# Emitting an attention-and-MoE kernel's own plan under the framework's manual schedule

## The chip, the core and the metric

One core of one Trainium2 chip. The time is device microseconds of one execution of the program, from its first to its last instruction with what the launch adds around them; the median of several executions counts. The engines are named as in the profile: PE (matmuls; PEld is its weight loads), DVE (vector), ACT (scalar), POOL and SP, of which SP issues nearly all input transfers and POOL some.

## The reference

Two stages, all in float32. First an attention over 32 memory slots, for 8 batches of 8 heads with 576 tokens of 64 elements:

```python
a = softmax(phi, over tokens)                    # phi: 8 x 8 x 576 x 32
k_m, v_m = a^T k, a^T v                          # 32 x 64 for each head
attn = softmax(q k_m^T / 8, over the 32 slots)
x = attn v_m                                     # to 4608 x 512
```

Then a feed-forward layer on the 4608 rows: `h = x @ w_in` (512 to 2048), `g = relu(h)**2`, and `out = g @ w_out` (2048 to 512).

## The kernel before

**The work.** The kernel never forms x. For each batch and each slice of 256 columns of w_in it multiplies v_m into w_in once (the tile `vw`; L679 for batches 0 and 1, L698 for the others), so that `h = attn @ vw`. A number that must be exact to float32 is kept as a high and a low part, each in the reduced-width float32 type of the matmuls, and each product is three matmuls: high by high, high by low, low by high. So each `h` tile is evacuated by several steps: relu into `r` (L811 on ACT or L812 on DVE), the high part `gh` of its square (L813, ACT), the square itself in `r` (L815 ACT or L816 DVE), and the low part `glo` (L817, DVE). The last 64 of the 576 tokens go the same way through the small tiles `gl` (L814 on ACT, L818 on DVE). The second product adds `gh` and `glo` times w_out into four PSUM banks `acc` (L842, L843 with `gh`; L845 with `glo`), and the 64 tokens left over of two batches into `accl` (L868).

**A step** is one batch and one block of 128 of the 2048 hidden columns: 12 matmuls of `h` (tile `h{step}_1` has 320 tokens, `h{step}_0` has 256) and 12 of `acc`. There are 8 x 16 steps. For batches 2 to 7, two batches form a pair n = 1, 2, 3. In the first batch of a pair every second step also makes a slice s = 0 to 7 of `vw` for both batches: two groups of six matmuls, `pvw{n}_{s}_0` and `pvw{n}_{s}_1` (`vw_step`, L689). Both groups write the same single PSUM bank (tag `pv`), so the second must wait until the first has been read out of it. The reading out is four copies on ACT (L328, called with `src`) and four subtractions on DVE (L707), each on 64 of the 128 partitions:

```python
pw = pt("pv", f"pvw{n}_{s}_{hh}")
...
op({"PE": 720}, mm, [t, vh, vl], [pw], lead=True)
for hf in (0, 1):
    pr = slice(64 * hf, 64 * hf + 64)
    for x in (0, 1):
        ...
        op({"ACT": act(SL)}, ..., [pw], [(V, (hh, 0, hf))], lead=True)
        vec({"DVE": tt(SL)}, ..., [pw, (V, (hh, 0, hf))], [(V, (hh, 1, hf))], ...)
```

**The start** is different. The weights come as 8-byte numbers, and 32 pieces of 512 KB (`raw`, L402) are decoded into high and low parts by a chain that goes back and forth between DVE (L404, L406, L407, L409, L418) and ACT (L405, L408, L328). A raw buffer is loaded again when its L409 has run. The decoding runs beside the steps of batches 0 and 1, up to about 200 us.

**What sets the order.** The kernel doesn't emit its instructions as it builds them. Each is an `Op` of a `Plan` (class at L58) with a cost on each engine that could take it and with the ops on which it depends. `plan.order()` schedules all ops on a model of five engines and a DMA wire, forward and backward in turns, and gives a list sorted by planned start (`o.start`). The costs are formulas such as `tt(n) = 68 + 1.04 n` ns for a DVE operation on n columns and `act(n) = 35 + 0.96 n` on ACT; a reader of a tile depends on its writer, but two readers of one tile don't depend on each other. The ops are then emitted in that list's order (L977). Under the framework's ordinary mode, this order is only the priority with which the framework's scheduler lists each engine's instructions, by a model of its own; it may put an instruction behind later ones. The framework sets all semaphores. It also lets no two engines use one PSUM bank at the same time, in the order in which the accesses were emitted.

**Fillers.** Where the plan sees PE idle before an op, `fill` (L350) emits matmuls on a tile of zeros, one for each 360 ns of the planned gap. They write the bank `idle` (L354) or, when `acc` is in use, add zero to a live bank (L356). There are 54 of them, nearly all before the first step.

Of the kernel before, what the change touches and what calls it, by code (L numbers as in the profile page):

```python
# [33 lines left out]
FILL = 360.0  # L34
# [240 lines left out]
def tile_attention_moe(  # L275
# [41 lines left out]
    plan = Plan()  # L317
# [32 lines left out]
    def fill(n):  # L350

        for _ in range(n):
            if idle is not None and not live:
                nc.tensor.matmul(idle, zero.broadcast_to([P, P]), zero.broadcast_to([P, 512]), start=True, stop=True)  # L354
            elif live:
                nc.tensor.matmul(live[min(live)](), zero.broadcast_to([P, P]), zero.broadcast_to([P, 512]), start=False, stop=False)  # L356
# [3 lines left out]
                            fill=0.0, base=0, channel_multiplier=1)  # L360
    nc.gpsimd.affine_select(out=bd, in_=bd, pattern=[[32, 4]], compare_op=ALU.is_ge,
                            fill=0.0, base=31, channel_multiplier=-1)
# [611 lines left out]
        for ff in range(NFF):  # L974
            step(pos[b1, ff])

    for o in plan.order():  # L977
        if o.left == "PE":
            fill(int(o.gap / FILL))
        o.fn(o.left)  # L980


# [28 lines left out]
```

## Time and profile before

| | us |
|---|---|
| median of 3 runs (all) | 807.02 (806.92, 807.02, 810.13) |
| the profiled execution | 805.84 |
| its span, first to last instruction | 804.0 |
| PE busy | 769.0 (96%) |
| DVE busy | 570.4 (71%) |
| ACT busy | 376.8 (47%) |
| mean granted PE clock | 0.983 |

The profiled execution is 1.84 us longer than its span, and 1.18 us shorter than the median of the runs. PE's busy time is a union of overlapping matmuls, so small stalls between two matmuls do not show in it; they show in the distance between two starts, or in the chain that ended last, where a piece reaches from one end to the next. In timeline rows the columns are start, duration, engine, line, operation and tiles, with the count, and in square brackets the engine's idle time before it and what ended that. Tile names in the profile have no numbers.

### The profile page before, as it was taken

To read this page: it belongs to the slowest core of one execution; us is meant where nothing else is said; L and a number is where in the kernel's file an instruction comes from. 1 tells how busy PE (TensorE), PEld (TensorE's weight loads), DVE (VectorE), ACT (ScalarE), POOL (GpSimd) and SP (SyncE) were. 2 spreads that over 40 slices of the span, in tenths; PEclk is the share of its full clock that TensorE was granted. 3 is DMA by queue.
4 is the path that set the end of the run, shared out by engine and by line. 5 is a ranking of instruction groups with operands and counts; after the bars stand their busy time and mean duration, and the time that the engine had idled before them with its cause. 6 is when DMAs were issued, how large, how long until landed. Compare 5 with 4: busy or idle time off the path is not lost.

```text
span 804.0 us, 13239 instructions
## 1 busy us (share of the span) xinstructions
PE 769.0 (96%) x4944; PEld 652.0 (81%) x4944; DVE 570.4 (71%) x1262; ACT 376.8 (47%) x857; POOL 54.1 (7%) x95
## 2 busy tenths in 40 slices
PE   9678899999999999999999999999999999999994
PEld 5467788888788888888888888888888888888883
DVE  3897988895659667966669667967759667974541
ACT  1566676675454444532443444533444444542220
POOL 4111102120100100010000100010000100000000
PEclk9789999999999999999999999999999999999998
DMA  6976754566554333421454523421424523110001
GB/s 194 291 243 227 247 185 156 206 217 185 164 142 134 119 99 97 126 50 52 125 152 123 132 88 98 136 52 38 120 82 112 139 82 104 31 34 20 1 8 58
DMA packets 91779, 97.89 MB, mean 122 GB/s; under 512 B 23812, under 2 KB 79108, under 8 KB 91716
## 3 DMA queue, kind: packets, MB, share of 16 engines
q1 hardware_dynamic: 82980, 81.55, 34.3%
q0 software_dynamic: 8736, 15.50, 6.6%
q8 instruction: 39, 0.64, 0.3%
q14 instruction: 24, 0.20, 0.1%
HBM read 79.17 MB, written 17.83 MB: 121 GB/s over the span
## 4 chain that ended last, share of the span: by engine, by line
PE 81%; DMA 7%; DVE 5%; ACT 4%; issue 1%; SPq 0%; ACTq 0%; DVEq 0%
PE h L807 22%; PE acc L842 13%; PE acc L845 13%; PE acc L843 13%; PE accl L868 5%; PE pvw L698 5%; DMA raw<-in_moe_w_out_dram 3%; PE psc L736 3%; PE pkv L484 3%; DMA raw<-in_moe_w_in_dram 2%; PE idle L354 1%; PE pvw L679 1%; DMA phi<-in_phi_dram 1%; ACT vw L328 1%; DVE vw L707 1%
## 5 line engine op out<-in xcount | busy, mean ns | idle before, releaser
L807 PE MATMUL h<-ath,vw 128*128 128x256 f32 (+1 forms) x1024 | 212.1, 302 | 2.9 <-ACT r L811 1.7
L842 PE MATMUL acc<-wo,gh 128*128 128x512 f32 x512 | 207.3, 406 | 2.1 <-ACT wo L328 1.0
L843 PE MATMUL acc<-wo,gh 128*128 128x512 f32 x512 | 201.7, 395 | 0.0
L807 PEld LDWEIGHTS h<-ath,vw 128*128 128x128 f32 x1024 | 171.4, 191 | 17.7 <-ACT r L811 2.2
L845 PE MATMUL acc<-wo,glo 128*128 128x512 f32 x512 | 155.3, 397 | 1.6 <-DVE glo L817 1.6
L842 PEld LDWEIGHTS acc<-wo,gh 128*128 128x128 f32 x512 | 96.7, 189 | 22.4 <-ACT gh L813 1.5
L328 ACT CAST vw<-pvw 64x256 fp32r<-64x256 f32 (+1 forms) x202 | 73.4, 378 | 85.2 <-PE pvw L698 55.9
L807 PE MATMUL h<-atl,vw 128*128 128x320 f32 (+1 forms) x512 | 111.2, 297 | 0.0
L813 ACT ACTIVATE gh<-r 128x512 fp32r<-128x512 f32 x128 | 80.8, 631 | 64.9 <-DVE r L812 53.2
L843 PEld LDWEIGHTS acc<-wo,gh 128*128 128x128 f32 x512 | 96.8, 189 | 16.3
L845 PEld LDWEIGHTS acc<-wo,glo 128*128 128x128 f32 x512 | 91.0, 189 | 17.2 <-DVE glo L817 2.6
L812 DVE TENSOR_SCALAR r<-h 128x256 f32<-128x256 f32 (+1 forms) x125 | 56.0, 448 | 60.4 <-PE h L807 59.5
L707 DVE TENSOR_TENSOR vw<-pvw,vw 64x256 fp32r<-64x256 f32 x192 | 78.5, 419 | 26.6 <-ACT vw L328 23.5
L817 DVE TENSOR_TENSOR glo<-r,gh 128x512 fp32r<-128x512 f32 x128 | 87.4, 683 | 6.4 <-ACT r L815 3.7
L811 ACT ACTIVATE r<-h 128x320 f32<-128x320 f32 (+1 forms) x131 | 53.7, 413 | 66.4 <-PE h L807 65.0
L807 PEld LDWEIGHTS h<-atl,vw 128*128 128x128 f32 x512 | 83.3, 191 | 0.4
L814 ACT ACTIVATE gl<-r 128x64 fp32r<-128x64 f32 x128 | 32.5, 254 | 78.6 <-DVE r L812 76.9
L816 DVE TENSOR_TENSOR r<-r 128x576 f32<-128x576 f32 x53 | 40.1, 757 | 26.7 <-ACT gh L813 24.3
L868 PE MATMUL accl<-wo,gl 128*128 128x512 f32 x192 | 53.0, 393 | 0.0
L815 ACT ACTIVATE r<-r 128x576 f32<-128x576 f32 x75 | 51.3, 684 | 1.8
L868 PEld LDWEIGHTS accl<-wo,gl 128*128 128x128 f32 x192 | 35.0, 188 | 7.2 <-ACT o L328 0.5
L698 PE MATMUL pvw<-wi,VTh 128*128 128x256 f32 x192 | 38.8, 292 | 1.5 <-issue 0.8
(142 smaller groups left out, 839.4 us busy)
## 6 DMA issues: line engine op xcount, KB each, us to landing
wi<-w_in_hi SPq DMA_DIRECT2D x56, 256.0 KB
wi<-w_in_lo SPq DMA_DIRECT2D x56, 256.0 KB
KV<-in_k_dram SPq DMA_DIRECT2D x32, 256.0 KB
KV<-in_v_dram SPq DMA_DIRECT2D x32, 256.0 KB
raw<-in_moe_w_in_dram SPq DMA_DIRECT2D x16, 512.0 KB
raw<-in_moe_w_out_dram SPq DMA_DIRECT2D x16, 512.0 KB
q<-in_q_dram SPq DMA_DIRECT2D x24, 288.0 KB
out_dram<-o POOLq DMA_DIRECT2D x20, 256.0 KB, 7.9
```

The source lines that it names most:

```text
L328: nc.scalar.copy(o, i) if e == "ACT" else ENG[e].tensor_copy(o, i)
L698: nc.tensor.matmul(pw()[:, x * SL:(x + 1) * SL], l()[:, 2 * hh + x, :], w(r, x), start=(i == 0), stop=(i == 2))
L707: vec({"DVE": tt(SL)}, lambda e, V=V, pr=pr, src=src: nc.vector.tensor_sub(V()[pr, 1, hh, :], src(), V()[pr, 0, hh, :].bitcast(F32)), [pw, ...
L807: nc.tensor.matmul(p()[:, 0:n], V()[:, l, hh, c0:c0 + P], x()[:, hh, cs], start=(i == 0), stop=(i == 5))
L811: op({"ACT": act(n), **({} if b < 2 else {"DVE": tt(n)})}, lambda e, cs=cs, n=n, p=p: nc.scalar.activation(r()[:, cs], p()[:, 0:n], AF.Rel ...
L812: else nc.vector.tensor_scalar(r()[:, cs], p()[:, 0:n], 0.0, None, ALU.max), [p], [(r, h)])
L813: op({"ACT": act(SM)}, lambda e: nc.scalar.activation(gh(), r()[:, 0:SM], AF.Square), [r], [gh])
L817: vec({"DVE": tt(SM)}, lambda e: nc.vector.tensor_sub(glo(), r()[:, 0:SM], gh().bitcast(F32)), [r, gh], [glo])
L842: nc.tensor.matmul(a(), gh()[:, c], t()[:, 0], start=f0, stop=False)
L843: nc.tensor.matmul(a(), gh()[:, c], t()[:, 1], start=False, stop=False)
L845: nc.tensor.matmul(a(), glo()[:, c], t()[:, 0], start=False, stop=f1)
L868: nc.tensor.matmul(a(), G()[:, l, :], t()[:, w], start=(ff == 0 and n == 0), stop=(ff == NFF - 1 and n == 2))
```

## The change

One `with` is put around the emission. The instructions, their engines, their tiles and their data dependences are the same; what changes is who orders them. Each engine now gets its instructions in the order in which they are emitted, which is the plan's.

```diff
-    for o in plan.order():
-        if o.left == "PE":
-            fill(int(o.gap / FILL))
-        o.fn(o.left)
+    with tc.manual_schedule():
+        for o in plan.order():
+            if o.left == "PE":
+                fill(int(o.gap / FILL))
+            o.fn(o.left)
```

Three places show what moves. **PE between the two `pvw` groups** of slice 4 in pair 1 (steps 38 and 39; `vw`, `ath` and `atl` are the operands of `h`). Before, from the last two `acc` matmuls that follow `pvw1_4_0` to the first row of `pvw1_4_1`:

```order
L845 MATMUL acc2_0_0_3118<-wo21_1098,glo37_3399 128x512
L845 MATMUL acc2_0_1_3128<-wo21_1098,glo37_3399 128x512
L807 MATMUL h38_1_3433<-ath2_2933,vw1_0_3_3305 128x320 x2
L807 MATMUL h38_1_3433<-atl2_2978,vw1_0_3_3305 128x320 x2
L807 MATMUL h38_1_3433<-ath2_2933,vw1_0_3_3305 128x320 x2
L807 MATMUL h38_0_3450<-ath2_2933,vw1_0_3_3305 128x256 x2
L807 MATMUL h38_0_3450<-atl2_2978,vw1_0_3_3305 128x256 x2
L807 MATMUL h38_0_3450<-ath2_2933,vw1_0_3_3305 128x256 x2
L845 MATMUL acc2_0_2_3135<-wo21_1098,glo37_3399 128x512
L845 MATMUL acc2_0_3_3156<-wo21_1098,glo37_3399 128x512
L807 MATMUL h39_1_3468<-ath2_2933,vw1_0_3_3305 128x320 x2
L698 MATMUL pvw1_4_1_3441<-wi1_4_1_3307,VTh10_2336 128x256 x2
```

The same place on PE under the plan's order:

```order
L845 MATMUL acc2_0_0_3120<-wo21_1100,glo37_3401 128x512
L845 MATMUL acc2_0_1_3130<-wo21_1100,glo37_3401 128x512
L807 MATMUL h38_1_3435<-ath2_2935,vw1_0_3_3307 128x320 x2
L807 MATMUL h38_1_3435<-atl2_2980,vw1_0_3_3307 128x320 x2
L807 MATMUL h38_1_3435<-ath2_2935,vw1_0_3_3307 128x320 x2
L698 MATMUL pvw1_4_1_3443<-wi1_4_1_3309,VTh10_2338 128x256 x2
L698 MATMUL pvw1_4_1_3443<-wi1_4_1_3309,VTl10_2344 128x256
```

The second group now stands ten matmuls earlier: the six of `h38_0`, two of L845 and the first two of `h39_1` are behind it instead of ahead. Ahead of these rows stand four matmuls of L842 and L843 right behind `pvw1_4_0`, in both orders. The same move stands at slices 3, 4, 5 and 6 of all three pairs, twelve times.

**DVE at the same place**, from the first subtraction that reads `pvw1_4_0`. Before:

```order
L707 TENSOR_TENSOR vw1_0_4_3417<-pvw1_4_0_3408,vw1_0_4_3417 64x256
L707 TENSOR_TENSOR vw1_1_4_3423<-pvw1_4_0_3408,vw1_1_4_3423 64x256
L812 TENSOR_SCALAR r38_3448<-h38_1_3433 128x320
L707 TENSOR_TENSOR vw1_1_4_3423<-pvw1_4_0_3408,vw1_1_4_3423 64x256
L707 TENSOR_TENSOR vw1_0_4_3417<-pvw1_4_0_3408,vw1_0_4_3417 64x256
L812 TENSOR_SCALAR r38_3448<-h38_0_3450 128x256
L812 TENSOR_SCALAR r39_3490<-h39_1_3468 128x320
```

And under the plan's order:

```order
L707 TENSOR_TENSOR vw1_0_4_3419<-pvw1_4_0_3410,vw1_0_4_3419 64x256
L707 TENSOR_TENSOR vw1_1_4_3425<-pvw1_4_0_3410,vw1_1_4_3425 64x256 x2
L707 TENSOR_TENSOR vw1_0_4_3419<-pvw1_4_0_3410,vw1_0_4_3419 64x256
L812 TENSOR_SCALAR r38_3450<-h38_1_3435 128x320
L707 TENSOR_TENSOR vw1_0_4_3419<-pvw1_4_1_3443,vw1_0_4_3419 64x256
L812 TENSOR_SCALAR r38_3450<-h38_0_3452 128x256
```

All four subtractions of the first group now stand ahead of the relu of `h38_1`, which stood between the second and the third of them.

**PE before the first step** (`pmx1_0`, `patl0`, `pat0_1` are transposes in the attention of batches 0 and 1; `idle` is the fillers' bank). Before:

```order
L645 MATMUL pat0_1_493<-ident_63,S0_1_442 128x128 x4
L469 MATMUL pmx1_0_537<-ident_63,mx1_0_528 128x128
L653 MATMUL patl0_520<-ident_63,rest0_237 128x128
L807 MATMUL h0_0_542<-ath0_376,vw0_0_0_491 128x256 x2
L807 MATMUL h0_0_542<-atl0_480,vw0_0_0_491 128x256 x2
```

And under the plan's order, from the end of a row of five fillers that follows `patl0`:

```order
L354 LDWEIGHTS zero_68
L354 MATMUL idle_74<-zero_68 128x512
L469 MATMUL pmx1_0_539<-ident_63,mx1_0_530 128x128
L354 LDWEIGHTS zero_68
L354 MATMUL idle_74<-zero_68 128x512
L807 MATMUL h0_0_544<-ath0_378,vw0_0_0_493 128x256 x2
```

Before, the ordinary mode had put 26 of the fillers at the very start, ahead of the first real matmul (`pmx0_0`), 27 more before `pat0_0`, and none behind that. Now 13 stand at the start, and 9, 9, 5 and 1 of them stand before `pvw0_0_0`, `patl0`, `pmx1_0` and `h0_0`. On ACT, in nearly all steps, `gl` (L814) stood before `gh` (L813), and now stands behind it. On SP a few loads change places in groups of two to four.

## The prediction

> **What bounds the kernel now.** I read the page first, then the stretches of the span, then the chain that ended last in the stretch where the change moves most, then the timeline there.
>
> ```profile
> PE 769.0 (96%) x4944; PEld 652.0 (81%) x4944; DVE 570.4 (71%) x1262; ACT 376.8 (47%) x857; POOL 54.1 (7%) x95
> ...
> PE 81%; DMA 7%; DVE 5%; ACT 4%; issue 1%; SPq 0%; ACTq 0%; DVEq 0%
> ```
>
> PE carries 81% of the chain. The stretches say where it doesn't (columns: stretch, length, busy time of PE, PEld, DVE, ACT and POOL with counts, granted clock, DMA share, GB/s):
>
> ```profile
> 0.00:160.00 160.00, 139.09 (x1083) 112.42 (x1084) 127.03 (x279) 97.18 (x207) 28.51 (x49) 0.94 0.69 218
> ...
> 285.00:330.00 45.00, 44.87 (x257) 39.29 (x257) 33.25 (x76) 21.95 (x55) 0.00 (x0) 1.00 0.39 119
> ...
> 693.00:794.00 101.00, 100.14 (x537) 87.21 (x535) 56.18 (x118) 29.83 (x68) 0.00 (x0) 1.00 0.06 20
> ```
>
> PE is idle for 20.9 us of the first 160 and for under 1 us in each of the others shown, of which 285 to 330 us is a stretch with `pvw` groups, and 693 to 794 has none. So behind the decoding an order can hardly win anything. It can only lose, by making PE wait for an engine that was early enough before. In the first 160 us it can do either.
>
> **The twelve `pvw` places.** The chain in steps 37 to 39 of pair 1 (columns: start, length, what):
>
> ```profile
> 293.44 0.71 PE pvw L698 x6
> 294.15 0.23 PE acc L842
> ...
> 294.84 0.23 PE acc L843
> 295.08 0.46 PE acc L845 x2
> 295.54 1.59 PE h L807 x12
> 297.13 0.47 PE acc L845 x2
> 297.60 0.29 PE h L807 x2
> 297.89 0.90 PE pvw L698 x6
> ...
> 303.75 0.71 PE pvw L698 x6
> ```
>
> Between the two groups PE has four matmuls of 0.23, then 0.46, 1.59, 0.47 and 0.29: 3.73 us of work. Two matmuls of 320 columns take 0.29, so the six of `h38_1` take 0.88. Under the plan's order only the four of 0.23, the 0.46 and `h38_1` are left between the groups: 0.92 + 0.46 + 0.88 = 2.26 us. The bank's reading out must fit into that. The timeline of it, from PE's first row behind `pvw1_4_0` to its first of `pvw1_4_1`, with a row of `glo` ahead for its duration:
>
> ```profile
> 293.26 0.69 DVE L817 TENSOR_TENSOR glo<-r,gh 128x512 fp32r<-128x512 f32 x1
> ...
> 293.99 0.40 PE L842 MATMUL acc<-wo,gh 128*128 128x512 f32 x1
> ...
> 294.19 0.63 ACT L328 CAST vw<-pvw 64x256 fp32r<-64x256 f32 x2 [2.60 <-PE pvw L698]
> ...
> 294.85 0.42 DVE L707 TENSOR_TENSOR vw<-pvw,vw 64x256 fp32r<-64x256 f32 x1 [0.77 <-ACT vw L328]
> ...
> 295.30 0.37 ACT L328 CAST vw<-pvw 64x256 fp32r<-64x256 f32 x1 [0.48 <-DVE vw L707]
> ...
> 295.70 0.42 DVE L707 TENSOR_TENSOR vw<-pvw,vw 64x256 fp32r<-64x256 f32 x1 [0.43 <-ACT vw L328]
> ...
> 296.15 0.37 ACT L328 CAST vw<-pvw 64x256 fp32r<-64x256 f32 x1 [0.48 <-DVE vw L707]
> ...
> 296.45 0.49 DVE L812 TENSOR_SCALAR r<-h 128x320 f32<-128x320 f32 x1 [0.33 <-PE h L807]
> ...
> 296.97 0.77 DVE L707 TENSOR_TENSOR vw<-pvw,vw 64x256 fp32r<-64x256 f32 x2
> 296.97 0.26 ACT L814 ACTIVATE gl<-r 128x64 fp32r<-128x64 f32 x1 [0.45 <-DVE r L812]
> ...
> 297.77 0.42 DVE L812 TENSOR_SCALAR r<-h 128x256 f32<-128x256 f32 x1
> ...
> 297.84 0.48 PE L698 MATMUL pvw<-wi,VTh 128*128 128x256 f32 x2
> ```
>
> ACT and DVE take turns in this bank: each copy from the third on waits for a subtraction, and the subtractions for the copies. The emission order, which sets these turns, is unchanged, so they stay. From 293.99 to 297.84 are 3.85 us; PE has work for 3.73 of them and waits 0.12. With the relu L812 behind the subtractions, as the second pair of orders shows, the last pair of subtractions starts at 296.15 + 0.37 + 0.03 (the step from ACT to DVE in the rows above) = 296.55, ends 0.77 later at 297.32, and PE starts at 297.42 (0.10 after, as in these rows). So the bank is free for PE 3.43 us after 293.99, and PE has work for 2.26: it waits 1.17 us instead of 0.12, **1.05 us more**. Nothing takes PE's place behind that wait: `h38_0`, which waits for nothing new, is queued behind it. The period from one slice to the next, 303.75 - 293.44 = 10.31 us, becomes about 11.4. At twelve places: **+12.6 us**. Between ends: 0 if the turns went away; and 1.45 each, 17.4 in all, if a further wait of 0.4 follows. That could be the four L845 that need `glo`, for all eight subtractions and both relus of the next step are ahead of it on DVE. From the start of the second group, PE comes to them after 0.71 + 0.71 + 0.46 + 0.88 + 0.71 and eight of 0.23, 5.3 us; DVE, behind the group's 0.71, has two copies (0.63), a subtraction (0.42), two copies (0.63), three subtractions (0.42 + 0.77), two relus (0.49 + 0.42) and `glo` (0.69), 5.2 us and the steps between. That is on the edge, and I take no further wait.
>
> At slice 7 the same bank gets easier, since its subtractions are no longer parted by a transpose, and at slice 2 and at the scores (L736) some matmuls come nearer to what they wait for, by up to five `acc` matmuls of 0.23, 1.15 us. All waits of PE for other engines behind the decoding are small now:
>
> ```profile
> PE acc L845 <- DVE glo L817: 0.9, 3, 0.3
> ...
> PE pvw L698 <- DVE vw L707: 0.6, 2, 0.3
> ```
>
> These two, 1.5 us, are most of what can be won back there; what can be lost is about four such places of 1.15. I take **+1.5** (bounds -2 and +5).
>
> `gl` behind `gh` delays the square, which waits for both, by one `gl`: 0.26 us. PE's work between `gh` and `glo` covers it: the row of L845 above shows no wait over 0.3. Where that cover is gone, it is the further 0.4 above. The extra semaphore instructions on DVE cost nothing I can see, with DVE at 33.25 of 45 us.
>
> **The start.** Two things pull one way. First, the fillers at the very start hold the first real transpose up:
>
> ```profile
> 0.99 7.72 PE idle L354 x26
> ...
> 4.47 1.24 DVE L467 TENSOR_REDUCE mx<-phi 128x128 f32<-128x640 f32 x1 [3.50 <-DMA phi<-in_phi_dram]
> ...
> 4.81 3.41 PEld L354 LDWEIGHTS <-zero 128*128 128x128 bf16 x16 [0.28 <-issue]
> ...
> 8.55 0.27 PE L469 MATMUL pmx<-ident,mx 128*128 128x128 f32 x1
> ...
> 21.12 8.93 DMA phi<-in_phi_dram
> ```
>
> `mx` is done at 5.71, `pmx` comes at 8.55. With 13 fillers instead of 26 (nine until 4.81, four more at 3.41 / 16 = 0.21 each) PE is free at 5.7, so this chain is up to 2.7 us earlier. But behind it the chain goes through loads (the last row, of the chain: 8.93 us on one), so only a part of it will last. Second, the clock:
>
> ```profile
> 27.00:45.00 18.00, 7.86 (x43) 6.80 (x43) 16.10 (x37) 8.60 (x18) 3.43 (x5) 0.64 0.95 295
> ...
> 44.94 1.64 PE h L807 x6
> ...
> 47.04 2.82 PE h L807 x12
> ```
>
> From 27 to 45 us PE is granted 0.64, and the first `h` tiles take 1.64 and 2.82 where the same counts take 0.71 and 1.59 later: 2.16 us. The 24 fillers that now stand in this stretch can save that. The Trainium skill (TensorE: Matmul & The Clock Gate, The HAM clock gate) says that an idle window of about 3.4 us halves the clock and a busy one of that length restores it. By it the nine fillers ahead of `patl0`, slowed, would be long enough to restore the clock; the row's 0.64, a mixture, agrees with two states, and the sum would be the same 2.16.
>
> Against these: on DVE the subtraction L418 of the first w_out piece, which ran in a gap, now stands behind an L404 that waits for its load:
>
> ```profile
> 37.08 0.68 DVE L418 TENSOR_TENSOR wo<-work,wo 128x512 fp32r<-128x512 f32 x1
> 39.01 0.43 DVE L404 TENSOR_SCALAR work<-raw 128x512 f32<-128x512 f32 x1 [1.25 <-DMA raw<-in_moe_w_out_dram]
> ```
>
> That puts 0.68 into the chain. On ACT the copies L408 come later, just ahead of where DVE's L409 needs them, in many of the 32 pieces; each L409 that waits keeps its raw buffer, and with it the next load. One such wait may cost an ACT operation of 0.6 to 0.7 (as L418's 0.68 on DVE), and the chain passes some eight loads of raw: 0 to 5.5 us. The gains are at most 2.7 + 2.16 = 4.9, the losses at most 0.7 + 5.5 = 6.2. I take **0** (bounds -5 and +6).
>
> **Sum.** 12.6 + 1.5 + 0 = +14.1 us. The profiled execution takes 805.84, its span 804.0; 805.84 + 14.1 = 819.9. The median of the runs stands 1.18 above that execution, so the median to expect is 807.02 + 14.1 = **821.1**.
>
> **The rivals.**
>
> *No wait at the bank* (chance 0.10, no change). If copies and subtractions ran side by side, the second group would be in time: one copy of 0.37 and four subtractions at 0.77 / 2 make 1.9 us, and with the 0.2 and 0.1 at its ends 2.2, within the 2.26. Then the 12.6 is gone, and so is 12 x 0.12 = 1.4 of now: 805.84 + 1.5 - 1.4 = 805.9, in medians 807.1. The "0.48 <-DVE vw L707" on the copies speaks against it. The Trainium skill (PSUM — Partial Sum Buffer, PSUM bank collisions raise a hardware error) has such a rule: engines in different quadrants of one bank may work at the same time, and these accesses take half the partitions each. The trace doesn't use it; every copy from the third on waits.
>
> *The start wins more than the rest loses* (chance 0.10, faster). PE is idle 20.9 us of the first 160. If the fillers and the plan's order won 4.9 there and the places at the bank cost nothing, the time is 805.84 - 4.9 - 1.4 - 2 = 797.5, in medians 798.7; if the bank costs its 12.6, the start would have to win over 18. The DMA at 0.95 and DVE at 16.10 of 18 us in the first stretch speak against it.
>
> *The decoding falls behind as well* (chance 0.10, slower). Each engine is now held by its first instruction that waits, and DVE and ACT wait for each other four times in each piece. If the start costs its 6.2 and the bank its 17.4 with 5 at the scores: 805.84 + 28.6 = 834.4, in medians 835.6.
>
> **How the numbers follow.** My forecast has 0.70, with 813 to 830 for its own range: 807.02 + 12.6 - 2 - 5 = 812.6, and 807.02 + 12.6 + 1.5 + 6 = 827.1 with half of the 4.8 that the twelve places can cost beyond 12.6. A measurement of this kernel can tell about 0.5% from no change, 4 us. The forecast and the third rival are slower by more: 0.80. No change 0.10, faster 0.10. For 8 in 10, the range takes in the first rival (807.1) but for its lower edge, leaves out the second, and takes in the lower part of the third: 806 to 832.
>
> **What would show it.** Right: at slices 3 to 6 of each pair, PE's wait before L698 for DVE L707 is 1.0 to 1.3 us, twelve times, the period is 11.3 to 11.7 us, and the stretch from 285 on takes about 4 us longer than 45. The first `pmx` starts near 5.8 us, and the first `h` rows take near 0.7 and 1.6. The loops from 693 us on keep their length. Wrong: no wait over 0.3 at L698, a period near 10.3, or a step 0 that starts more than 6 us earlier or later than at 44.94.

## The result

The changed kernel takes 817.89 us in the median of 4 runs (816.85 to 819.8), the kernel before 807.63 (806.92 to 810.13): a ratio of 1.0124, 95% interval 1.0094 to 1.0154. Its profiled execution takes 818.21 us, its span 816.4, which is 12.4 more than before. On the page PE's busy time is

```profile
PE 774.8 (95%) x4939; PEld 650.5 (80%) x4944; DVE 568.3 (70%) x1262; ACT 367.1 (45%) x857; POOL 54.2 (7%) x95
...
PE 69%; DVE 15%; ACT 5%; issue 5%; SPq 2%; DMA 2%; DVEq 0%; ACTq 0%
```

The chain now leaves PE for 31% of its way. Stretches of the changed kernel (columns as in the prediction; the loops from 693 us on now begin at 705.4):

```profile
0.00:160.00 160.00, 146.30 (x1126) 118.93 (x1132) 133.78 (x293) 101.03 (x219) 30.09 (x51) 0.96 0.72 227
285.00:330.00 45.00, 41.35 (x229) 34.74 (x228) 29.07 (x66) 19.07 (x49) 0.00 (x0) 1.00 0.37 107
...
705.40:806.40 101.00, 100.56 (x538) 87.35 (x536) 56.36 (x120) 28.29 (x68) 0.00 (x0) 1.00 0.06 19
```

In the first 160 us PE is busy for 7.2 us more than before: it is *ahead*. From 285 to 330 us it is busy for 3.5 less, and in the 101 us of the last loops all is as it was. Following single matmuls through both traces, by their place in the program, shows where the time changes hands (start of the first 320-column matmul of the step, us):

| step | before | changed | changed - before |
|---|---|---|---|
| 2 | 59.45 | 59.56 | +0.1 |
| 8 | 111.83 | 105.05 | -6.8 |
| 24 | 204.42 | 195.49 | -8.9 |
| 31, last before pair 1 | 238.18 | 228.86 | -9.3 |
| 57, behind pair 1's slices | 392.80 | 390.61 | -2.2 |
| 89, behind pair 2's slices | 574.73 | 580.48 | +5.7 |
| 112, behind pair 3's slices | 709.64 | 722.56 | +12.9 |
| 127, the last | 773.10 | 786.02 | +12.9 |

So two effects of opposite sign: 9.3 us won by step 31, nearly all of it from 60 to 205 us, and 22.2 us lost in the slices of the three pairs, 7 to 8 in each. Of these, 6.86, 6.94 and 6.90 lie between the second group of slice 2 and the first of slice 7, at the twelve places: 20.7 us, 1.72 each. The last 0.5 us between +12.9 and the spans' +12.4 are won behind step 127.

**At one of the twelve places.** The timeline of PE in the changed kernel, from the first group of slice 4 to that of slice 5:

```profile
285.86 0.40 PE L698 MATMUL pvw<-wi,VTh 128*128 128x256 f32 x2
...
286.57 0.40 PE L842 MATMUL acc<-wo,gh 128*128 128x512 f32 x1
...
290.00 0.47 PE L698 MATMUL pvw<-wi,VTh 128*128 128x256 f32 x2 [1.01 <-PE h L807]
...
293.68 0.50 PE L842 MATMUL acc<-wo,gh 128*128 128x512 f32 x1
...
294.02 0.40 PE L843 MATMUL acc<-wo,gh 128*128 128x512 f32 x1
...
297.88 0.40 PE L698 MATMUL pvw<-wi,VTh 128*128 128x256 f32 x2
```

From 286.57 to 290.00 are 3.43 us, the bank's reading out as forecast, for 2.26 us of work on PE. The profile names PE's own L807 as the releaser, which had long been done; the last subtraction L707 is what ends there (289.90). But the period is 297.88 - 285.86 = 12.02 us, not 11.4. The chain of waits shows why (start, length, what):

```profile
289.01 1.00 issue
290.00 0.96 PE pvw L698 x6
290.96 0.02 issue
290.99 0.37 ACT vw L328
...
291.37 0.38 ACT vw L328
...
291.77 0.43 DVE vw L707
...
292.22 0.37 ACT vw L328
...
293.87 0.43 DVE vw L707
...
294.33 0.82 DVE r L812 x2
...
295.19 0.70 DVE glo L817
...
295.93 1.20 PE acc L845 x4
```

Before, this stretch of the chain was PE's alone. Now it is a loop through three engines: second group, four copies and four subtractions in turns, the two relus of the next step queued behind them, `glo`, and the four L845 that need it. That takes 5.93 us. PE has less other work, and waits a little at L842 for `gh` (0.16) and more at L845 for `glo`; and after each of these two waits the next matmul starts 0.34 later (293.68 to 294.02) instead of 0.23. From the starts of single matmuls: 1.06 us more at the bank, 0.23 at L842, 0.40 at L845, and 0.03 that is not assigned, of 1.72. `gl` ahead of the square is not what makes `glo` late here: the square (L815 on ACT, 293.80 to 294.49) is done 0.70 before `glo` starts, and DVE is at the two relus until 295.15.

**From 60 to 205 us** the other sign is seen on ACT. In the kernel before, the waits of ACT from 45 to 175 us are

```profile
ACT raw L408 <- DMA raw<-in_moe_w_out_dram: 10.6, 6, 4.3
ACT raw L408 <- DMA raw<-in_moe_w_in_dram: 7.9, 9, 3.2
```

and over the whole span, of those who waited for `raw`,

```profile
ACT raw L408: 22.9, 19
```

In the changed kernel's lists neither line is there: ACT never stands at L408. The framework had listed L408, which needs only the load, up to 13 places earlier on ACT than the plan did, and one of the 32 by 91. ACT then stood at it until the load landed, and what was queued behind it, for which DVE and PE were ready, stood too. DVE's waits for ACT in the decoding (L407 for L405, L418 for L328) from 45 to 175 us were 3.7 + 2.4 + 1.8 = 7.9 us before; of these one line is left:

```profile
DVE work L407 <- ACT work L405: 0.4, 1, 0.4
```

Up to 1.7 us of the lead, half of 3.4, can be the clock: before, PE is granted 0.50 from 66.3 to 69.7 us, and in the changed kernel 1.00 from 41 us on.

### The profile page after: what moved, and what is told of

It is laid out like the page before. It is cut to its first block, busy times and chain, and to the rows that moved or that the text cites. A ratio compares the mean times of both kernels' runs of the same rounds, so it can differ in the third digit from the quotient of the medians.

```text
span 816.4 us, 13331 instructions
## 1 busy us (share of the span) xinstructions
PE 774.8 (95%) x4939; PEld 650.5 (80%) x4944; DVE 568.3 (70%) x1262; ACT 367.1 (45%) x857; POOL 54.2 (7%) x95
## 4 chain that ended last, share of the span: by engine, by line
PE 69%; DVE 15%; ACT 5%; issue 5%; SPq 2%; DMA 2%; DVEq 0%; ACTq 0%
PE h L807 18%; PE acc L845 12%; PE acc L842 11%; PE acc L843 11%; PE accl L868 5%; PE pvw L698 4%; ACT vw L328 3%; DVE vw L707 3%; PE pkv L484 2%; PE psc L736 2%; DVE glo L817 1%; DVE work L407 1%; DVE r L812 1%; DVE work L409 1%; DMA q<-in_q_dram 1%
## 5 line engine op out<-in xcount | busy, mean ns | idle before, releaser
L807 PE MATMUL h<-ath,vw 128*128 128x256 f32 (+1 forms) x1024 | 211.1, 299 | 0.8 <-ACT r L811 0.6
L842 PE MATMUL acc<-wo,gh 128*128 128x512 f32 x512 | 209.2, 409 | 0.0
L843 PE MATMUL acc<-wo,gh 128*128 128x512 f32 x512 | 201.3, 393 | 0.0
L807 PEld LDWEIGHTS h<-ath,vw 128*128 128x128 f32 x1024 | 169.3, 189 | 15.3 <-ACT r L811 1.1
L845 PE MATMUL acc<-wo,glo 128*128 128x512 f32 x512 | 157.3, 400 | 2.2 <-DVE glo L817 0.7
L813 ACT ACTIVATE gh<-r 128x512 fp32r<-128x512 f32 x128 | 80.9, 632 | 130.3 <-DVE r L812 119.0
L328 ACT CAST vw<-pvw 64x256 fp32r<-64x256 f32 (+1 forms) x202 | 73.5, 378 | 126.8 <-PE pvw L698 82.9
L707 DVE TENSOR_TENSOR vw<-pvw,vw 64x256 fp32r<-64x256 f32 x192 | 78.7, 420 | 69.7 <-ACT vw L328 67.9
L842 PEld LDWEIGHTS acc<-wo,gh 128*128 128x128 f32 x512 | 96.5, 188 | 20.8 <-ACT gh L813 1.9
L843 PEld LDWEIGHTS acc<-wo,gh 128*128 128x128 f32 x512 | 96.5, 188 | 16.5
L807 PE MATMUL h<-atl,vw 128*128 128x320 f32 (+1 forms) x512 | 109.4, 295 | 0.0
L845 PEld LDWEIGHTS acc<-wo,glo 128*128 128x128 f32 x512 | 90.4, 189 | 22.2 <-DVE glo L817 8.1
L807 PEld LDWEIGHTS h<-atl,vw 128*128 128x128 f32 x512 | 82.3, 189 | 0.0
L698 PE MATMUL pvw<-wi,VTh 128*128 128x256 f32 x192 | 38.1, 291 | 15.1 <-PE h L807 10.1
L815 ACT ACTIVATE r<-r 128x576 f32<-128x576 f32 x75 | 51.4, 685 | 1.8
L698 PEld LDWEIGHTS pvw<-wi,VTh 128*128 128x128 f32 x192 | 31.1, 189 | 23.6 <-PE h L807 14.9
```

The lines of the kernel that those rows point to most:

```text
L328: nc.scalar.copy(o, i) if e == "ACT" else ENG[e].tensor_copy(o, i)
L698: nc.tensor.matmul(pw()[:, x * SL:(x + 1) * SL], l()[:, 2 * hh + x, :], w(r, x), start=(i == 0), stop=(i == 2))
L707: vec({"DVE": tt(SL)}, lambda e, V=V, pr=pr, src=src: nc.vector.tensor_sub(V()[pr, 1, hh, :], src(), V()[pr, 0, hh, :].bitcast(F32)), [pw, ...
L807: nc.tensor.matmul(p()[:, 0:n], V()[:, l, hh, c0:c0 + P], x()[:, hh, cs], start=(i == 0), stop=(i == 5))
L813: op({"ACT": act(SM)}, lambda e: nc.scalar.activation(gh(), r()[:, 0:SM], AF.Square), [r], [gh])
L842: nc.tensor.matmul(a(), gh()[:, c], t()[:, 0], start=f0, stop=False)
```

## The experiments

Each was timed against the kernel before on its own chip; the ratio carries over from one comparison to the next. "On the first scale" is that ratio times 807.63.

| run | median us | ratio (95% interval) |
|---|---|---|
| changed kernel | 817.89 | 1.0124 (1.0094 to 1.0154) |
| e1 plan's order up to step 24 only | 795.92 | 0.9868 (0.9842 to 0.9894) |
| e2 plan's order from step 24 only | 827.67 | 1.0283 (1.0231 to 1.0334) |
| e3 before, L408 not moved ahead | 798.57 | 0.9900 (0.9875 to 0.9925) |
| e4 changed, L408 moved ahead | 822.51 | 1.0207 (1.0165 to 1.0248) |
| e5 e1 and the plan's order on PE | 824.08 | 1.0200 (1.0167 to 1.0232) |
| e6 e1 and the plan's order on DVE, ACT | 810.98 | 1.0050 (1.0026 to 1.0074) |
| e7 changed, copies ahead of subtractions | 815.63 | 1.0089 (1.0060 to 1.0117) |
| e8 changed, second group later | 838.96 | 1.0378 (1.0337 to 1.0420) |
| e9 changed, plan knows the turns | 795.12 | 0.9825 (0.9773 to 0.9877) |
| e10 changed, no fillers | 823.33 | 1.0174 (1.0129 to 1.0219) |
| e11 e9's plan, framework's order | 805.36 | 0.9993 (0.9967 to 1.0018) |

**e1 and e2: the two halves apart.**

```diff
+    order = plan.order()
+    cut = plan.ops[first].start
     with tc.manual_schedule():
-        for o in plan.order():
+        emit(o for o in order if o.start < cut)
+    emit(o for o in order if o.start >= cut)
```

`first` is the number of step 24's first op, `emit` the old loop with its fillers. In e2 the `with` is around the second part instead.

> The plan's order up to the planned start of step 24 (before that step every piece of the weights has been decoded), the framework's order behind it. On every engine the first part then reads as in the changed kernel and the second as in the kernel before. Theory (two effects with opposite signs: the start wins 9.3 us, the 128 steps behind it lose 22.2): 807.6 - 9.3 = 798.3 us. Rival one (the start's lead is only lent, and is given back in the loops of pairs 1 to 3 whatever their order): 807 us, with the lead shrinking from 240 us on. Rival two (my forecast's start, which wins nothing): 807 to 809 us, with no lead at step 24.

> The other half: the framework's order up to step 24, the plan's order behind it. Theory: no lead at step 24, and the loss of pairs 1 to 3 in full, 807.6 + 22.2 = 829.8 us, with the period of slices 3 to 6 at 12.0 us. Rival (the loss needs the early start, because loads or evacuations of the first part reach into the second): about 818 us or less.

e1 is 1.3% faster than before, 797.0 on the first scale; its lead at step 24 is 10.7 us (193.76) and 10.4 at the last step: nothing is given back. e2 is 2.8% slower, 830.5, with no lead at step 24 (204.63) and 23.0 lost at the last step. The rivals of a lent lead, of a start that wins nothing and of a loss that needs the early start are out; the halves add up to the changed kernel.

**e3 and e4: L408 alone.** In e3 a call pins each L408 of the kernel before behind the ACT operation that was emitted just ahead of it. In e4 the 32 are put back, in the changed kernel, to the places on ACT that the framework had given them: `earlier` puts each behind as many other ACT ops as stood ahead of it before.

```diff
-lambda e: nc.scalar.activation(low(), low(), AF.Copy, scale=2.0 ** -29)
+lambda e: tc.keep_in_program_order(nc.scalar.activation(low(), low(), AF.Copy, scale=2.0 ** -29))
```

```diff
-        for o in plan.order():
+        for o in earlier(plan.order()):
```

> The kernel before under the framework's ordinary mode, but the 32 copies L408 of the decoding (ACT, the low words of a raw buffer) may not move ahead of the ACT operation emitted just before them. Behind step 24 all orders are those of the kernel before, and PE's order is nearly the same at the start too. Theory (what the start wins comes from ACT no longer standing at L408 until a load lands, 22.9 us of idle time in the kernel before and none in the changed one): ACT's idle time at L408 goes to under 3 us, PE is ahead by 6 to 9 us at step 24, and the time is 798 to 802 us. Rival (the fillers and the clock, or PE's and DVE's order, win it): 806 to 808 us.

> The changed kernel, all orders as in it, but the 32 copies L408 stand on ACT where the framework had them in the kernel before (13 places further ahead at most but for one piece, which is far ahead). Theory: ACT stands at L408 again until loads land, 15 to 25 us in all, most of the lead of 9.3 us at step 24 is gone, and the time is 824 to 828 us. Rival (fillers, clock, or the other engines' order): 817 to 819 us, the idle time at L408 notwithstanding.

e3: no idle time of ACT at L408 at all, step 24 at 196.96, 7.5 us ahead of before, and 799.6 us on the first scale. PE's order at the start is nearly that of before, with its 26 fillers ahead of the first transpose, so neither fillers nor PE's order make this. The framework moved some of DVE's decoding along with L408, so e3 does not tell the two apart.

e4 changes ACT's order alone, and gives back part: from step 2 to step 24 PE takes 139.9 us, where the changed kernel takes 135.9 and the kernel before 145.0. But it comes to step 2 by 2.0 us earlier than the changed kernel, so that of the lead of 8.9 us at step 24 it still has 7.1, where most was expected to be gone. The time, 824.3 on the first scale, is at the lower edge of what was expected; in the traces e4 is only 2.5 us behind the changed kernel at the last step. So the reason given for it was at most half right. ACT stands at L408 for

```profile
  DMA raw<-in_moe_w_in_dram: 2.9, 2
  DMA raw<-in_moe_w_out_dram: 0.8, 2
```

3.7 us, not 15 to 25. What did come back is DVE's wait for ACT:

```profile
DVE work L407 <- ACT work L405: 3.6, 4, 2.3
```

So an L408 listed early can harm in two ways: by ACT's wait for the load, and by its own 0.68 us ahead of an L405 for which DVE waits. Why the loads were nearly all there in time in e4 is open. With e3 and e4 together, the places of L408 are shown to cost time, with up to 7.5 us in e3; how much of it is ACT's order alone, and how much DVE's that moves with it, is not.

**e5 and e6: which engine's order loses the time behind step 24.**

```diff
-    emit(o for o in order if o.start >= cut)
+    with tc.manual_schedule(engines={mybir.EngineType.PE}):
+        emit(o for o in order if o.start >= cut)
```

In e6 the engines are DVE and Activation (ACT).

> Times here are on the scale of the first comparison (before 807.6, changed 817.9). The plan's order on all engines up to step 24, and behind it on PE alone; DVE and ACT are left to the framework there. With PE fixed it still puts the relu of the step between the second and the third subtraction of the first group, so that bank is read out in 3.85 us and not in 3.43, while PE has 2.26 us of work. Theory (PE comes to the bank too early, and that is where the loss starts): the wait ahead of the second group is 1.5 to 1.6 us, the period 12.0 to 12.5, the time 817 to 823 us. Rival (the loss needs the plan's order on DVE and ACT, where the relus of the next step and its low part are queued behind the subtractions): 796 to 805 us, a period of 10.3 to 11.0.

> The complement: the plan's order on all engines up to step 24, behind it on DVE and ACT alone; PE is left to the framework, which now puts the second group eight matmuls later than the plan, but behind six of them instead of ten. Theory (a loop of engines: second group, its four copies, its four subtractions, two relus queued behind them, the low part, the four L845 that wait for it; 5.9 us from the group's start to the first L845): PE has only 4.1 to 4.5 us of other work there, so the wait moves from the bank to the L845, 1.2 to 1.6 us each, and the time is 808 to 818 us. Rival (the second group's place on PE alone is the cause): 796 to 800 us, no wait over 0.3 us.

e5: 823.8 on the first scale, just beyond the 823 expected, with a period of 299.53 - 287.10 = 12.43 us, and at the bank

```profile
287.10 0.40 PE L698 MATMUL pvw<-wi,VTh 128*128 128x256 f32 x2
...
291.67 0.48 PE L698 MATMUL pvw<-wi,VTh 128*128 128x256 f32 x2 [1.43 <-issue]
...
299.53 0.40 PE L698 MATMUL pvw<-wi,VTh 128*128 128x256 f32 x2
```

From the first L842 behind the first group (287.81) to 291.67 are 3.86 us, the 3.85 of the kernel before, for PE's 2.26. So PE's order alone brings the loss. e6: 811.7, a period of 11.66; DVE and ACT in the plan's order lose as well, with PE free to adapt. The wait has moved, though not to L845 as expected:

```profile
PE h L807 <- DVE r L812: 6.6, 9, 0.7
```

`h39_0` uses the PSUM bank of `h38_0`, which a relu has yet to read that is queued behind a subtraction of the second group. Each of the two orders loses by itself; "PE's place of the second group alone" is out.

**e7 and e8: the turns, and the place of the group.**

```diff
 e7, slices 3 to 6, first group: in the list, the subtractions behind the last of the four copies
-  copy copy sub copy sub copy sub sub
+  copy copy copy copy sub sub sub sub
 e8, slices 3 to 6: in the list, on PE
-  h38_1  pvw1_4_1  h38_0  acc acc  h39_1  h39_0
+  h38_1  h38_0  acc acc  h39_1  pvw1_4_1  h39_0
```

> The changed kernel, but at the twelve places the four subtractions of the first group are emitted behind its four copies, and not among them. No engine's order changes: ACT and DVE only take fewer turns in the bank. Theory (the turns make the reading out long): it takes about 3.0 us instead of 3.43, PE's wait ahead of the second group falls from 1.16 to about 0.75, the loop behind it moves up by as much, the period is 11.6, and the time 12 x 0.4 less, 813 us. Rival (both engines may be in the bank at once, and the wait has another cause): 818 us and a wait of 1.16.

> The changed kernel, but at the twelve places the second group stands behind the first six matmuls of the next step on PE (14 matmuls later, some 2 us of work); ACT's order is the same, and on DVE one relu passes one subtraction. Theory (the loop of e6 sets the period, and it starts with the second group): the wait at the bank is gone, but the group starts about 1 us later, the copies, subtractions, relus and the low part with it, and PE waits at L842 and L845 instead: the period is about 13, the time 826 to 831 us. Rival (the second group's place on PE alone is the cause): 797 to 806 us.

e7: no engine's order differs from the changed kernel's, and yet PE's wait falls:

```profile
290.49 0.48 PE L698 MATMUL pvw<-wi,VTh 128*128 128x256 f32 x2 [0.73 <-PE h L807]
...
298.36 0.40 PE L698 MATMUL pvw<-wi,VTh 128*128 128x256 f32 x2
```

(1.01 in the same row before this edit), and the period is 298.36 - 286.62 = 11.74 us instead of 12.02. So the turns make the wait, and the 0.28 saved at the bank is saved in the period. It is less than the 0.4 that I expected, and the interval of the ratio overlaps that of the changed kernel: the period decides here, not the median.

e8: the wait at the bank is gone, and the kernel is slower than any other, 838.2 on the first scale, beyond the range given. PE waits at L842 instead:

```profile
PE acc L842 <- ACT gh L813: 23.5, 12, 2.0
```

ACT's order is that of the changed kernel, with the second group's copies ahead of `gh`; a later group makes later copies and a later `gh`. The mechanism is the one expected, but its price was under-estimated: a period is 13.4 us (12.2 at slice 6) where PE keeps its full clock, and 13.8 to 14.5 in five of the twelve, in which the granted clock falls to 0.50 for 3.41 us right behind such a wait. The changed kernel has no such fall there. Moving one instruction on the engine that waits does not mend a loop.

**e9 and e11: a plan that knows the turns.** In `vw_step` the four copies are made first (y = 0), and then each subtraction `o` (y = 1) depends on all of them:

```diff
-        for hf in (0, 1):
-            for x in (0, 1):
+        for y, hf, x in [(y, hf, x) for y in (0, 1) for hf in (0, 1) for x in (0, 1)]:
...
+            [(o.deps.add(c), c.users.append(o)) for c in copies if c not in o.deps]
```

> The changed kernel, manual order throughout, but the plan is told of the turns in the bank: each of the four subtractions of a group depends on all four copies of it, and the plan orders everything anew. It now puts the second group behind h38_0 (six matmuls later than in the changed kernel, 2.97 us of work behind the first group), ACT's high part ahead of the second group's copies, and the relu of the next step ahead of its subtractions. Theory (the loss is the plan's missing rule: it places the second group and the relus as if both engines could read the bank at once): the waits at the bank fall to 0 to 0.4 us each, the low part isn't late any more, the period is 10.3 to 10.8, and the time, with the start's lead kept, 797 to 803 us. Rival (the plan's costs are off in other places as well, and a fixed order can't follow the engines as the framework's does): 810 to 818 us.

> The plan of e9, with the turns in it, but emitted under the framework's ordinary mode, as in the kernel before. Theory (two separate causes: the copies L408, which the framework's order puts ahead on ACT whatever the plan, and the turns, which the framework's order took into account anyway): ACT stands at L408 for some 20 us again, and the time is 803 to 809 us. Rival (a plan that knows the turns is enough in either mode): 795 to 799 us.

e9 has the lowest median, 1.75% under the kernel before, which is 793.5 on the first scale and better than expected. It can't be told from e1, though: the intervals overlap, and both spans are 793.6 us. From step 36 to step 44, four slices, it takes 43.5 us (275.63 to 319.12), the kernel before 43.9 and the changed one 51.8. From 240 us on, the list of PE's waits is one line, and the stretch is full again:

```profile
PE acc L842 <- ACT gh L813: 1.7, 6, 0.4
```

```profile
285.00:330.00 45.00, 44.74 (x253) 39.22 (x252) 34.17 (x76) 22.79 (x61) 0.00 (x0) 1.00 0.41 120
```

e11 has the same plan under the framework's order: no gain (0.9993), no loss in the slices (43.4 us for the same four), and ACT at L408 again:

```profile
  DMA raw<-in_moe_w_in_dram: 15.0, 11
  DMA raw<-in_moe_w_out_dram: 12.6, 7
```

So there are two separate effects, and e9 keeps the gain of the start while it undoes the loss in the slices.

**e10: the fillers.** `fill` emits none; all else as in the changed kernel.

> The changed kernel without its 54 fillers; all other orders are the same. Theory (the lead comes from ACT's copies L408, and the fillers' places matter little): the granted clock from 27 to 45 us falls, the first steps start up to 2 us later, and the time is 816 to 821 us on the scale of the first comparison (changed 817.9). Rival (the 24 fillers that the plan's order leaves in front of the first steps keep the clock up, and that makes the lead): the lead of 9.3 us at step 24 is gone, 825 to 827 us.

It lies between the two, 821.7 on the first scale: fillers are worth about 4 us to the changed kernel (4.5 at step 127 by the traces), 1.8 of it by step 2 (61.36), and the lead over the kernel before at step 24 is 5.3 us instead of 8.9. They matter, but most of the lead doesn't hang on them. Without them the first `h` tiles run at half speed: in this row the two matmuls take 0.63, at their full pace 0.40, and they start 0.213 us apart instead of 0.12:

```profile
47.86 0.63 PE L807 MATMUL h<-atl,vw 128*128 128x256 f32 x2
```

The granted clock of e10 from 36 to 42 and from 45 to 52 us (the figure behind POOL's count):

```profile
36.00:42.00 6.00, 3.76 (x16) 3.38 (x16) 5.17 (x14) 2.69 (x6) 0.40 (x2) 1.00 0.95 339
45.00:52.00 7.00, 5.18 (x24) 4.69 (x28) 6.32 (x12) 3.84 (x8) 0.39 (x1) 0.53 0.31 89
```

In the changed kernel the second of these stretches has 1.00. The 0.53 is a reading, the 1.00 of the first row is not: the trace of e10 has no record of the clock ahead of 42.01 us, and a time without one counts as 1.00. The matmuls of 256 columns start 0.213 us apart there too (38.50 to 40.42), so PE ran at half pace, and the fall of the clock that was expected from 27 to 45 us shows in the pace and not in the figure. The Trainium skill (TensorE: Matmul & The Clock Gate, The HAM clock gate) says that a PE idle for a window of about 3.4 us is put to half its clock. The trace agrees: from 42.01 to 45.42 us PE has one transpose of 0.33 us, and then the clock is at 0.50 for 6.83 us; and the records of the clock in the traces of before, the changed kernel and e10, but for the last of each, last 3.41 us or a whole multiple of it.

## Why the prediction was right, and where it wasn't

The number (+14.1 us, measured +12.4 in the spans and 10.3 in the medians) and the sign were right, but two of the three terms were outside their bounds, with opposite signs, and nearly cancelled. That the sum came out near is luck.

- **Twelve places, +12.6: right mechanism, too small; 20.7.** The first link held to the hundredth: 3.43 us of reading out, 2.26 us of work, 1.17 of wait. What failed is "I take no further wait". I had set PE's 5.3 us against DVE's 5.2 "and the steps between", and left those steps at nothing; they made `glo` ready at 5.9. With the two late links, 0.23 and 0.40, a place costs 1.72, beyond the 1.45 that I named as the upper end. In e6 and e8 the wait moves to other links, which fits one loop. The delay by `gl`, which I counted to that further wait, cost nothing at the place followed.
- **The rest behind the decoding, +1.5: right in size.** 22.2 - 20.7 = 1.5; where these 1.5 us lie was not followed.
- **The start, 0 with bounds -5 and +6: wrong; -9.3.** Up to step 2 it holds, +0.1. The first `pmx` came earlier, at 6.51 and not at 5.8: the last four of the 13 fillers took 0.43 us each like the first nine, not 0.21. Step 0 began 1.6 us later than before (46.58), which the faster first tiles made good by step 2. What failed is the sentence on the copies L408. I took it that later on ACT means later for L409, a loss of up to 5.5 us. That an instruction ahead in ACT's queue can stand there, and hold up those behind it, is in the trace of before: its list of all waits, read before the prediction, has ACT at L408 for 14.1 and 8.8 us. I built on PE's waits alone, where this appears only at third hand. How much of the 9.3 us it makes is bounded by e3 (7.5) and not settled by e4.
- **The rivals.** "No wait at the bank" was answered by the first link, and by e7: the turns are real. "The start wins more" had the sign of the start right, but for reasons (fillers, clock) that e10 gives 3.6 of the 8.9 us at step 24; on the whole it did not come, since the bank cost more than the start won, the condition that it names itself. "The decoding falls behind" was wrong in sign: under the fixed order the decoding was faster.
- **What would show it.** The wait at L698 and the loops' length came as said; the period of 11.3 to 11.7 did not (12.0), and steps 36 to 44 take 51.8 us where they took 43.9, 8 us more and not 4.

## What to carry to other kernels

An order of instructions is judged at the waits at the head of *every* engine's queue, ACT's and DVE's too, and not only at those of the engine that is busy: an instruction that is ready early by its data (here a copy that needs only a load) is the one that a scheduler may list too early. A hand-made plan put in force exactly brings its model's errors with it; the wait shows at one link (the bank), but the cost is that of the loop it belongs to, so that shifting the waiting instruction alone made it worse (e8), and giving the model the missing rule mended it (e9). Where a change to an order touches several stages, forecast and test each by itself: here +22 and -9 us looked like one change of +1.2%.

## What the runs showed of the hardware that was not expected

After a wait at L842 or L845 the first matmul of 512 columns is followed by the next 0.33 to 0.34 us later, not 0.23 (all 24 places in the changed kernel), so that each such wait costs a tenth of a microsecond beyond what it lasts. Waits shorter than those 3.41 us can cost the clock as well: in e8, with 1.8 to 2.0 us a period, the granted clock fell to 0.50 five times, each within 0.7 us of a wait's end, while the changed kernel, with its 1.2 us at the bank, keeps 1.00 from 41 us to the last loops. And a granted clock of 1.00 at the start of a span can be the absence of a record. In e10, from 36 to 42 us, the matmuls show it:

```profile
38.93 0.63 PE L679 MATMUL pvw<-wi,VTl 128*128 128x256 f32 x2
```
